# Routed attention with a SoLU block on one Trainium2 core: one pass of cluster products for two-token pairs, and a new order of all engines

## The chip, the cores and the metric

The kernel runs on one core of one Trainium2 chip. The metric is device time in microseconds, the median of repeated runs. The engines are PE (TensorE matmul; PEld is its weight load), DVE (VectorE), ACT (ScalarE), POOL (GpSimd) and SP (SyncE, which issues nearly all DMAs).

## The reference

Four batches of eight heads, 768 tokens of 64 numbers each. Every query and key is assigned to one of 16 centroids of its head, and a query attends only to keys of its own cluster. The result, 3072 rows of 512, goes through a block of width 1024. All inputs and the output are float32.

```python
q_assign = np.argmax(np.einsum('bhsd,hcd->bhsc', q_n, c_n), axis=-1)   # normalised q, k, centroids
k_assign = np.argmax(np.einsum('bhsd,hcd->bhsc', k_n, c_n), axis=-1)
mask = q_assign[:, :, :, None] == k_assign[:, :, None, :]
scores = np.where(mask, scale * np.matmul(q, k.transpose(0, 1, 3, 2)), -1000000000.0)
attn = np.exp(scores - np.max(scores, axis=-1, keepdims=True))
attn = attn / (np.sum(attn, axis=-1, keepdims=True) + 1e-09)
x = np.matmul(attn, v).transpose(0, 2, 1, 3).reshape(3072, 512)
h = x @ w_in
sm = softmax(h); solu = h * sm
ln = (solu - mean(solu)) / np.sqrt(var(solu) + 1e-06) * g_ln
return ln @ w_out
```

## The kernel before

Work goes by *pairs*: a batch `b` and two neighbouring heads, `b.p`, sixteen in all. For each pair the 64 numbers of a head lie along partitions, and below them one-hot marks of the token's cluster are appended, so that one product of marked keys and marked queries gives score plus a bonus for equal clusters; the exponential with a bias then does the masking. The marks of a pair's second head need their own rows, and marks of the other head there must be blank.

Steps have short names, followed by pair, operand (0 query, 1 key), head of the pair and half where there are any:

- `ld`, `lv`, `lo`, `li`, `lg`: loads of q and k, of v, w_out, w_in, g_ln. `tp`: tokens turned by PE into a bank of the PSUM region `hreg` (batch 0 only; the other batches are turned by `xt` on DVE). `xa`, `xb`: copies of what was turned to SBUF, tile `xt`. `ca`: cast of a head's part to the bfloat16 tile `qk`.
- `cl`: products of the turned tokens with the centroids into the PSUM tile `csc`. `tb` turns them back (`cst`), `mx` takes the largest of 16, `oh` makes the one-hot marks, `ot` turns these (`oht`), `pl` places a part of them into `qk` (a copy on POOL or DVE, or a DMA by SP), `bl` blanks a strip of the second head's key marks.
- `S`: one bank of scores (1 to 4 products); `E`: its exponential on ACT; `V`: products with v; `N`: division by the sum. A bank of scores goes to a ring of three PSUM tiles `sps`, or, for some early ones, to a bank of `hreg`.
- `ptx`, `tx`: x turned (by PE and copy, or by DMA); `h`: product with w_in into `hreg`; `hm`, `ex`, `u`: its largest, the exponential, the product h times exponential; `bn`, `ag`, `at`, `al`: the statistics and the scale `alpha`; `ptu`, `tu`: u turned; `y`: product with w_out; `sc`: scaling by alpha; `ou`, `oz`: the store.
- `su`, `me`, `ce`: the mean over rows of g_ln times w_out (DVE sums, a PE product) and w_out less it, which goes to `w_out_c`, the operand of every `y`. `wi`: casts of w_in. `cp`, `cb`, `cq`, `cf`: centroids turned, and their two forms kept as weights. `wm`, `fl`: idle products of PE during the opening.

Batch 0 is loaded with tokens contiguous in a partition. Its first pair goes by halves; its other three (`twelve` in the code) are loaded twelve tokens to a partition, so that a turn of 128 columns brings two tokens at once, one for each half of the partitions. Such a turned tile holds the even tokens of both heads in one half of the partitions and the odd ones in the other, and `cl` for these pairs uses weights with four variants `c_by_two` (part of the tokens by head), two products that add up for each of the four strips of `csc`, eight in all. An ordinary pair has four.

The order on every engine is written out by hand, as text: `ORDER["DVE"]` names kinds of step in the order in which they are issued, and each kind's steps come in the order in which they were added. `AWAY` lists steps that run on another engine than their default. An engine executes its own list strictly in order. Buffers that matter here: `hreg` has three banks, reused by `tp` and then by scores and `h`; unused parts of `w_out_c` hold small constants of the opening until `ce` fills it.

Of the kernel before, what the change touches and what calls it, by code (L numbers as in the profile page):

```python
# [10 lines left out]
F32 = mybir.dt.float32  # L11
BF16 = mybir.dt.bfloat16
# [10 lines left out]
class Weave:  # L23
# [6 lines left out]
        ld4 si ld3 lv lg ld3 lo lv lo ld2 lo2 lv ld6 lv ld8 li4 tx ld3 lv ld tx lv tu ld10 tx tu ld4  # L30
        tu lv ld ou lv ld3 tu ld3 ou ld8 ou2 ld2 tu ld5 tx lv2 ld pl tu ld10 tx ld5 ou2 tu lv tx lv
        tu ld9 ou tu ld4 lv2 ld4 pl tu ou tx ld3 tu tx ld4 ou tu2 ou lv tx lv ou pl3 tu3 ou tx2 ou2
        tu tx tu tx tu ou2 tx ou tu2 ou tu ou6
    """
    ORDER["POOL"] = """
        pl2 bl pl3 ca pl ca cv ca3 pl3 bl ca pl ca pl cv z2 pl3 ca bl z cv2 ca pl4 sg bl cv2 wi ca
        wi7 ca3 at pl4 z cv ca2 cv bl cv al pl2 ca3 at pl2 z bl ca3 al at al pl4 at ca cv ca cv ca
        cv al bl ca3 pl4 ca2 pl4 at2 pl2 bl ca cv pl al2 ca2 cv2 ca2 at cv ca4 al pl4 at2 cv bl cv3
        pl2 al pl2 ca2 bl ca at al ca pl2 cv2 pl ca3 al ca3 pl at2 pl3 al2 ca2 pl ca at cv pl cv at
        ca at cv al pl2 bl pl al at3 al2 at al2 at al at al2 at2 po at al3  # L40
    """
    ORDER["PE"] = """
        fl wm tp2 cp fl4 cl tp2 fl4 cl fl tp S2 cq S tp S tp S2 tp S tp2 S2 cl S V3 S2 tp3 S gt V3
        S2 tp2 S tp S2 cl S3 V3 S7 V3 S3 cl S3 V4 S5 V2 S V2 S4 V S2 V3 S cl S3 V2 S V S2 V S me S3
        V S V3 me S3 ptx V2 S2 cl V S V S5 V2 h4 S2 h V2 S3 h V2 S V2 S h S2 h S V S V2 S V S h S2 h
        V S2 V2 S y3 V S2 y S h2 S2 V2 h2 S2 cl S V S V2 S V S h S2 h S V S V S h y4 S3 V3 h2 S2 V2
        S h S2 V y S y3 S2 V2 S cl S V S V S V2 S2 y S y S2 V3 S2 y S V S y S2 V2 S h S2 V3 S2 cl S
        V3 S3 cl S2 V2 S V2 S h2 S3 h V S V S V2 y3 S2 y V S2 V h S2 V S h S V S h2 S3 h V2 S2 V4 h
        S3 y3 S2 V y S2 V3 S2 h2 S3 V2 cl S3 V2 h S2 h cl V2 S2 V2 S h S2 h2 S2 V3 y S y S y S y V S
        V2 S h2 S2 h2 S3 V3 S V y3 V y V S2 h S cl S3 V2 h S2 h V S2 V S cl V2 S3 y2 S V S V y2 h2  # L50
        S2 V2 S h2 S3 cl S V3 S V S2 y3 S2 V y V S h S2 h V2 S h2 S3 h V2 S y2 S V2 S2 V2 y2 S2 h3
        S3 V2 h2 V y S3 y3 V3 S3 h2 S2 cl S V S V S V2 S y2 h V S2 h V S2 h2 S2 V S V h V4 S2 y2 h
        S3 V2 h2 S2 V2 S y2 S2 h2 y2 S h2 S2 V2 y S V2 S y h2 S3 h2 S2 V4 y S3 h2 y V S2 h2 V S V S
        V y4 S2 V h4 S3 y V3 y S2 y2 h4 y S V3 y V y2 h ptx h y h2 y3 h2 y4 h2 ptu2 y8 ptu y4 ptu y4
    """
    ORDER["DVE"] = """
        cn xb cb tb mx oh ot pl2 tb mx oh ot xa3 cf ca bl cv tb mx oh ot ca2 xa gk su2 N tb mx xa oh
        cv ot su N su2 tb mx N oh su ot N xt2 N su tb mx su oh N xt2 N ce tx ce3 N ce4 hm N ot u N
        bn hm tb N mx oh bn ag ot u xt2 hm cv N bn u bn2 tb mx hm bn N oh ag2 u ot xt2 hm bn N sc u
        bn tb ag cv N xt mx oh xt ot sc N bl xt2 tb bn N mx ca tb N mx oh ot hm oh N ot u xt bn3 ag  # L60
        xt N ag hm sc N ca u bn2 xt bl sc hm ag N xt tb mx u tb oh ot N hm mx xt oh u bn2 ot N hm bn
        ag xt ca u N bn tb xt2 mx ag hm tb N bn2 oh ot u xt2 N hm tb mx oh N ag bn bl u mx bn ot N
        bn oh hm ot ag xt u N bn xt ag hm bn2 ag u sc N bl hm ca tb mx cv2 oh u ot N bn2 hm N bl u
        cv ag bn2 hm N bn u sc hm N u bn2 hm N bn ag u bn sc hm ag N bn u bn2 hm bn N ag2 u bn2 hm
        ag bn N ag2 u tx bn hm sc u bn2 hm tu2 bn ag2 u2 bn2 ag tu sc
    """
    ORDER["ACT"] = """
        wa xa2 ca2 xa2 xb ca4 E6 xa E2 xa E xa ca E3 xa3 E4 ca E2 xa E53 ex E13 ex E5 sc E3 ex E11
        ex E3 sc E5 ex E35 ex E15 ex E15 ex E9 ex E3 sc E8 ex sc E14 ex E sc E10 ex E5 sc E6 ex E5
        sc E3 ex ca E10 ex E9 ex E5 sc E2 ex E6 ex E7 ex E6 ex sc E5 ex E3 sc E ex sc ex sc ex sc2  # L70
        tu sc2 oz
# [3 lines left out]
        ca0.0.0.0.0 ca0.0.0.1.0 ca0.0.0.1.1 ca0.2.0.0 ca0.2.1.0 ca3.2.0.1 sc23.0 xa0.0.0.1 xa0.0.1.0  # L75
        xa0.1.1.1 xa0.2.0.0 xa0.2.0.1 xa0.2.1.0 xa0.2.1.1 xa0.3.0.0 xa0.3.1.0 xb0.0.1.1
    """.split(), "ACT"))
    AWAY.update(dict.fromkeys("""
        bl0.0.1 bl1.3 bl2.1 bl3.0 bl3.1 bl3.3 ca0.1.0.0 ca0.1.0.1 ca0.2.1.1 ca2.1.0.0 ca2.2.1.0
        ca3.0.0.1 ca3.3.1.0 cv0.0.0 cv0.1.0 cv1.1.0 cv1.2.0 cv3.1.1 cv3.2.1 cv3.3.0 pl0.0.0.0.1  # L80
        pl0.0.0.1.1 sc11 sc13 sc14 sc18 sc2 sc23.1 sc3 sc4 sc5 tu22.0
    """.split(), "DVE"))
    AWAY.update(dict.fromkeys("""
        ca0.0.1.1.1 pl0.0.0.0.0 pl0.0.0.1.0 pl0.0.1.0.0 pl0.0.1.1.0 pl1.0.0.0 pl1.0.0.1 pl1.0.1.0
        pl1.0.1.1 pl1.1.0.0 pl1.1.0.1 pl1.1.1.0 pl1.1.1.1 pl1.2.0.0 pl1.2.0.1 pl1.2.1.0 pl1.2.1.1
        pl1.3.0.0 pl1.3.0.1 pl1.3.1.0 pl1.3.1.1 pl2.0.0.0 pl2.0.0.1 pl2.0.1.0 pl2.0.1.1 pl2.1.0.0
        pl2.1.0.1 pl2.1.1.0 pl2.2.0.0 pl2.2.0.1 pl2.2.1.0 pl2.2.1.1 pl2.3.0.0 pl2.3.0.1 pl2.3.1.0
        pl2.3.1.1 pl3.0.0.0 pl3.0.0.1 pl3.0.1.0 pl3.1.0.0 pl3.1.0.1 pl3.1.1.0 pl3.1.1.1 pl3.2.0.0
        pl3.2.0.1 pl3.2.1.0 pl3.2.1.1 pl3.3.0.0
# [79 lines left out]
def kernel(  # L169
# [11 lines left out]
    nc = tc.nc  # L181
# [68 lines left out]
    def used(hh):  # L250

        return slice(0, D + NC_) if hh == 0 else slice(0, D + 2 * NC_)
# [222 lines left out]
    def clusters(b, p, hf, hh=None):  # L475

        lo, n = (0, HALF) if hf is None else (hf * HALF, QTR)
        if not hh:
            asg[b, p, hf, "csc"] = ps_m.tile([P, HALF], F32, name="csc", tag="m")
        csc = asg[b, p, hf, "csc"]  # L480
        if twelve(b, p):
            for c in range(4):
                i, part = divmod(c, 2)
                nc.tensor.matmul(csc[c * NB:(c + 1) * NB, :], c_by_two[:, p, 2 * part + hh, :],  # L484
                                 by_two(b, p, i)[:, hh].rearrange("p t n -> p (t n)"),
                                 start=(hh == 0), stop=(hh == 1), tile_position=(0, c * NB))
        for c in range(4) if not twelve(b, p) else ():
            i, part = divmod(c, 2)
            nc.tensor.matmul(csc[c * NB:(c + 1) * NB, :n], c_bd[:, p, :],  # L489
                             xts[b, p, i][:, lo + part * n:lo + (part + 1) * n],  # L490
                             tile_position=(0, c * NB))
        asg[b, p, hf, "n"] = n
# [25 lines left out]
    def assign_turn(b, p, hf):  # L518
        n = asg[b, p, hf, "n"]
        asg[b, p, hf, "oht"] = pr.tile([P, HALF], BF16, name="oht")  # L520
        nc.vector.transpose(asg[b, p, hf, "oht"][:, :n], asg[b, p, hf, "oh"][:, :n])  # L521
# [803 lines left out]
```

## Time and profile before

| what | value |
|---|---|
| median of three runs | 223.82 us (223.24, 223.82, 224.28) |
| span of the profiled execution, first to last instruction | 222.4 us |
| its whole time beside the span | not recorded; the median stands 1.4 us above the span |
| PE busy | 214.8 us (97%) |
| DVE, ACT, POOL busy | 199.1 (90%), 194.7 (88%), 126.6 us (57%) |
| granted PE clock over the span | 0.999 |

Busy time of an engine is the union of its instructions; that of PE includes the depth of its pipeline, so it overstates how full PE is. A row of the chain of work that ended last gives start, length and the engine, tile and line; "issue" is time in which the profile shows no cause. In a timeline row, "x6" merges six neighbouring instructions, and the bracket at its end gives the engine's idle time ahead of it and what ended it. "Q" names such as SPq are an engine's instruction queue.

### The profile page before, as it was taken

The numbers are of one execution on the slowest core, as the hardware profiler recorded it, in microseconds if no ns is written. First come the engines' busy times: TensorE is split into PE (matmuls) and PEld (weight loads), VectorE is DVE, ScalarE is ACT, GpSimd is POOL, SyncE is SP. The second block draws the span as 40 slices with busy tenths as digits, with TensorE's granted clock in tenths as the row PEclk, the third lists the DMA queues.
The fourth block names the chain that finished last, engine by engine and source line by source line (L and its number), as shares of the span: only waits on it lengthen the run. The fifth ranks groups of instructions, "written<-read, shape, count | busy, mean of one in ns | idle before, by whom it ended". The sixth has DMA issues, their size and how long they took to land.

```text
span 222.4 us, 6852 instructions
## 1 busy us (share of the span) xinstructions
PE 214.8 (97%) x2518; PEld 151.8 (68%) x2548; DVE 199.1 (90%) x363; ACT 194.7 (88%) x382; POOL 126.6 (57%) x252
## 2 busy tenths in 40 slices
PE   8999899999999999999999999999999999999993
PEld 7765577767777687777777666676767767665452
DVE  2789999999999999899989999999999979999891
ACT  3899999999999999999999989999999989795352
POOL 3189597759884986188837674783746101226131
PEclk9999999999999999999999999999999999999999
DMA  6998989797799979899999897998922928565623
GB/s 157 352 388 221 193 165 284 203 172 165 127 175 237 180 141 215 136 193 166 153 211 239 156 185 150 151 168 158 230 99 50 115 78 145 117 165 121 166 98 143
DMA packets 122433, 38.74 MB, mean 174 GB/s; under 512 B 111448, under 2 KB 117152, under 8 KB 122400
## 3 DMA queue, kind: packets, MB, share of 16 engines
q1 hardware_dynamic: 121680, 37.82, 79.8%
q10 hardware_dynamic: 720, 0.49, 0.7%
q8 instruction: 20, 0.33, 0.7%
q14 instruction: 13, 0.11, 0.1%
HBM read 23.11 MB, written 6.29 MB: 132 GB/s over the span
## 4 chain that ended last, share of the span: by engine, by line
PE 91%; DVE 3%; issue 2%; ACT 2%; DVEq 0%; ACTq 0%
PE sps L627 27%; PE hreg L744 18%; PE yps L813 17%; PE ops L654 16%; PE csc L489 4%; PE hreg L627 2%; PE idle_p L859 2%; PE csc L484 1%; PE hreg L403 1%; PE hreg L396 1%; ACT qk L468 1%; PE hreg L813 1%; ACT e L635 1%; DVE u L763 1%; DVE w_sum L598 1%
## 5 line engine op out<-in xcount | busy, mean ns | idle before, releaser
L635 ACT ACTIVATE e<-sps 128x512 bf16<-128x512 f32 (+1 forms) x276 | 143.2, 609 | 10.2 <-PE sps L627 9.8
L627 PE MATMUL sps<-qk 96*128 96x256 bf16 (+5 forms) x600 | 87.4, 263 | 0.7 <-ACT e L635 0.4
L627 PEld LDWEIGHTS <-qk 96*128 96x128 bf16 (+1 forms) x636 | 59.6, 121 | 24.5 <-issue 8.8
L654 PEld LDWEIGHTS <-e 128*128 128x128 bf16 x1152 | 49.9, 97 | 9.3 <-issue 1.9
L654 PE MATMUL ops<-v,e 128*128 128x65 bf16 x1152 | 54.3, 193 | 0.4 <-DVE x L679 0.4
L744 PE MATMUL hreg<-w_in_sb,xT 128*128 128x512 bf16 x177 | 48.3, 378 | 0.8
L813 PE MATMUL yps<-w_out_c,uT 128*128 128x512 bf16 x169 | 45.1, 379 | 0.8
L540 POOL COPY qk<-oht 32x384 f32<-32x384 f32 (+1 forms) x49 | 24.2, 494 | 21.5 <-DVE oht L521 15.7
L763 DVE TENSOR_TENSOR u<-e_sb,hreg 128x1024 bf16<-128x1024 bf16 (+1 forms) x25 | 29.1, 1169 | 2.7 <-ACT e_sb L756 2.1
L774 DVE BATCH_NORM_STATS2 bs<-u 128x6 f32<-128x512 bf16 x48 | 31.3, 677 | 0.0
L750 DVE TENSOR_REDUCE nmax<-hreg 128x1 f32<-128x1024 f32 x24 | 29.1, 1213 | 2.0 <-PE hreg L744 1.7
L756 ACT ACTIVATE e_sb<-hreg,nmax 128x1024 bf16<-128x1024 f32 x24 | 26.9, 1121 | 4.5 <-DVE nmax L750 4.4
L790 POOL TENSOR_SCALAR esq<-es,mv 128x1 f32<-128x1 f32 x24 | 8.3, 344 | 33.6 <-DVE mv L778 30.3
L813 PEld LDWEIGHTS <-uT 128*128 128x128 bf16 x200 | 18.0, 97 | 13.1 <-issue 0.3
L744 PEld LDWEIGHTS <-xT 128*128 128x128 bf16 x192 | 17.6, 97 | 11.3 <-ACT e L635 0.3
L472 POOL TENSOR_SCALAR qk<-xt 64x768 bf16<-64x768 f32 (+1 forms) x27 | 22.2, 823 | 3.5 <-DVE xt L444 1.7
L444 DVE STREAM_TRANSPOSE xt<-raw 128x768 f32<-128x768 f32 x24 | 22.2, 949 | 0.0
L470 POOL CAST qk<-xt 64x768 bf16<-64x768 f32 (+1 forms) x25 | 20.9, 836 | 1.2
L679 DVE TENSOR_TENSOR x<-ops,den 128x256 bf16<-128x256 f32 (+1 forms) x39 | 18.9, 486 | 1.3
L784 POOL TENSOR_SCALAR es<-esum 128x1 f32<-128x1 f32 x24 | 5.6, 236 | 20.9 <-ACT e_sb L756 20.4
L793 POOL TENSOR_TENSOR alpha<-esq,halves 128x1 f32<-128x1 f32 x24 | 13.8, 574 | 2.0
L830 ACT ACTIVATE y<-yps,alpha 128x512 f32<-128x512 f32 x15 | 10.4, 695 | 4.3 <-PE yps L813 3.0
(85 smaller groups left out, 206.9 us busy)
## 6 DMA issues: line engine op xcount, KB each, us to landing
vf<-in_v_dram SPq DMA_DIRECT2D x16, 384.0 KB, 4.6
out_dram<-y SPq DMA_DIRECT2D x23, 256.0 KB, 2.5
raw<-in_q_dram SPq DMA_DIRECT2D x50, 96.0 KB, 3.8
raw<-in_k_dram SPq DMA_DIRECT2D x50, 96.0 KB, 3.0
w_g<-in_moe_w_out_dram SPq DMA_DIRECT2D x4, 512.0 KB, 8.3
w_st<-in_moe_w_in_dram SPq DMA_DIRECT2D x4, 512.0 KB, 6.2
raw<-in_q_dram SPq DMA_DIRECT2D x3, 384.0 KB, 6.0
raw<-in_k_dram SPq DMA_DIRECT2D x3, 384.0 KB, 7.8
```

The source lines that it names most:

```text
L444: nc.vector.transpose(xt[:], raws[b, p, i][:].rearrange("p j c -> p (j c)"))
L472: VEC[e].tensor_scalar(dst, src, scalar1=inv_C, scalar2=1.0, op0=Alu.mult, op1=Alu.mult)
L540: ins = VEC[e].tensor_copy(dst.bitcast(F32), src.bitcast(F32).unsqueeze(1) .to_broadcast([NB, 2, n // 2]))
L627: ins = nc.tensor.matmul(sps_[n, k][:, c0:c0 + w], side(b, h // 2, 1, h % 2, keys)[r], side(b, h // 2, 0, h % 2, slice(s0 * P, s0 * P + w) ...
L635: ins = nc.scalar.activation(es[n, k][:, :w], sps_[n, k][:, :w], Act.Exp, scale=exp_scale, bias=-exp_scale)
L654: nc.tensor.matmul(opss[g][:, s, :VW], es[n, k][:, c0:c0 + P], v1[slot(b, h // 2)][:, h % 2, kt, :VW], start=(kt == 0), stop=(kt == n_t - 1))
L744: uses(nc.tensor.matmul(hreg[:, at(f, f2)[1], :], xTs[f][:, dc, :], w_in_sb[:, dc, f2 * FF2:(f2 + 1) * FF2], start=(dc == 0), stop=(dc == ...
L750: uses(nc.vector.tensor_reduce(ff[f, "nmax"][:], pair_of(f), axis=AXY, op=Alu.max, negate=True), *both(f))
L756: uses(nc.scalar.activation(ff[f, "e"][:], pair_of(f), Act.Exp, bias=ff[f, "nmax"][:], accum_out=ff[f, "esum"][:]), *both(f))
L763: uses(nc.vector.tensor_tensor(ff[f, "u"][:, r], ff[f, "e"][:, r], pair_of(f)[:, r], op=Alu.mult), *both(f)[r])
L774: nc.vector.bn_stats(ff[f, "bs"][:, f2, :], ff[f, "u"][:, f2, :])
L813: ins = nc.tensor.matmul(dst, ff[f, "uT"][:, at(f, f2)[0] * (n_fc // 2) + c, :], w_out_c[:, fc, cols], start=(fc == fcs[0] and turn == 0 i ...
```

## The change

For the three two-token pairs of batch 0, `cl` uses two weights (`c_two`, one for each head) and contracts over both token parities' partitions at once: a strip of `csc` belongs to a head's 32 marks, 16 for each parity, instead of to a parity's 32 marks, 16 for each head. Four products, one pass, no accumulation. `oh` writes the marks with the two parities parted: a strip `apart` of 128 x 768, zeroed once at the start, of which each group of 32 columns gets 16. `ot` then turns 768 columns instead of 384 into `turned_apart` (two buffers), and `pl` copies 16 rows by 768 marks into one head's rows instead of 32 by 384 into both heads'. Nothing needs a blank in these pairs, so their three `bl` are gone, and scores of their second heads contract over 80 rows instead of 96. Clearing of the four-variant mask (five POOL writes) becomes one write of `apart`; `cf` writes 256 columns instead of 512.

The text of `ORDER` is new for all engines and `AWAY` is new, as are some costs that the order does not depend on while it is written out. By the lists: SP issues 13 placements (before 5), POOL 51 (61), DVE 4 (2); DVE makes 8 of the twelve `xa` copies of the two-token pairs (5), ACT 4 (7); of casts DVE makes 4 whole ones and a half one (7 whole), ACT 3 whole and 1 half (3 and 6); DVE has 9 casts of v (7), 3 blanks (6) and 8 scalings of y with the two parts of the last (9 with one part). The first score bank must now stand behind all idle products.

```diff
     def clusters(b, p, hf):
         lo, n = (0, HALF) if hf is None else (hf * HALF, QTR)
-        if twelve(b, p):
-            for c in range(4):
-                i, part = divmod(c, 2)
-                nc.tensor.matmul(csc[c * NB:(c + 1) * NB, :], c_by_two[:, p, 2 * part + hh, :],
-                                 by_two(b, p, i)[:, hh].rearrange("p t n -> p (t n)"),
-                                 start=(hh == 0), stop=(hh == 1), tile_position=(0, c * NB))
+        csc = asg[b, p, hf, "csc"] = ps_m.tile([P, HALF], F32, name="csc", tag="m")
+        for c in range(4):
             i, part = divmod(c, 2)
+            if twelve(b, p):
+                w = c_two[:, p, part, :]
+                x = by_two(b, p, i)[:, part].rearrange("p t n -> p (t n)")
+            else:
+                w, x = c_bd[:, p, :], xts[b, p, i][:, lo + part * n:lo + (part + 1) * n]
+            nc.tensor.matmul(csc[c * NB:(c + 1) * NB, :n], w, x, tile_position=(0, c * NB))
...
     def assign_hot(b, p, hf):
+        if twelve(b, p):
+            dst = apart.rearrange("p (u a c) -> p a u c", u=2, c=NB)[:, :, :, :NC_]
+            src, top = (x.rearrange("p (a u) c -> p a u c", u=2)
+                        for x in (by_group(b, p, hf, "cst"), spread_max(b, p, hf)))
...
     def assign_turn(b, p, hf):
+        if twelve(b, p):
+            asg[b, p, hf, "oht"] = turned_apart[:, p % 2, :]
+            nc.vector.transpose(turned_apart[:, p % 2, :], apart)
+            return
...
         if twelve(b, p):
-            ins = VEC[e].tensor_copy(
-                every_other(b, p, i, part)[D:D + NB].bitcast(F32),
-                src.bitcast(F32).rearrange("p (t n) -> p t n", t=n_t // 2).unsqueeze(1)
-                .to_broadcast([NB, 2, n_t // 2, P // 2]))
+            dst = (side(b, p, i, part, slice(0, S))[D:D + NC_].bitcast(F32)
+                   .rearrange("p (t u n) -> p u t n", u=2, n=P // 2))
+            src = asg[b, p, hf, "oht"][r.start:r.start + NC_, :].bitcast(F32)
+            ins = VEC[e].tensor_copy(dst, src.rearrange("p (u t n) -> p u t n", u=2, n=P // 2))
...
     ORDER["PE"] = """
-        fl wm tp2 cp fl4 cl tp2 fl4 cl fl tp S2 cq S tp S tp S2 tp S tp2 S2 cl S V3 S2 tp3 S gt V3
+        fl3 wm fl tp2 cp fl tp cq tp fl2 cl fl tp2 fl cl tp fl tp2 S3 cl S2 tp S tp S2 tp S tp S gt
...
```

The places that matter for the time are shown as the engines' lists. First DVE in batch 0, where the second and third pairs' clusters and the last `xa` copies stand (L430 is `xa` before, L433 after; L595 and L598 are `su` before, L605 and L608 after; `w_out_c` as both result and source is the parted strip). Before:

```order
L430 COPY xt<-hreg 128x384
L588 COPY g_ln_115<-gps 128x8
L595 TENSOR_SCALAR w_sum<-w_g,g_ln_115 128x512
L598 SCALAR_TENSOR_TENSOR w_sum<-w_g,g_ln_115,w_sum 128x512
L666 RECIPROCAL den<-ops 128x6
L679 TENSOR_TENSOR x<-ops,den 128x2x3x64
L497 STREAM_TRANSPOSE cst<-csc 128x384
L510 TENSOR_REDUCE mx<-cst 128x24
L430 COPY xt<-hreg 128x384
L515 TENSOR_TENSOR oh<-cst,mx 128x384
```

After:

```order
L433 COPY xt<-hreg 128x384
L495 STREAM_TRANSPOSE cst<-csc 128x384
L527 STREAM_TRANSPOSE w_out_c<-w_out_c 128x768
L508 TENSOR_REDUCE mx<-cst 128x24
L676 RECIPROCAL den<-ops 128x6
L689 TENSOR_TENSOR x<-ops,den 128x2x3x64
L433 COPY xt<-hreg 128x384 x2
L521 TENSOR_TENSOR w_out_c<-cst,mx 128x12x2x16
L433 COPY xt<-hreg 128x384
L605 TENSOR_SCALAR w_sum<-w_g,g_ln_115 128x512
```

The first two `su` steps stood ahead of the last `xa` copy and now follow it; the wide turn stands ahead of it.

Second, ACT in the same place, from the first exponential on (L635 is `E` before, L645 after; L468 and L471 are casts). Before:

```order
L635 ACTIVATE e<-sps 128x384 x6
L430 COPY xt<-hreg 128x384
L635 ACTIVATE e<-sps 128x384 x2
L430 COPY xt<-hreg 128x384
L635 ACTIVATE e<-sps 128x384
L430 COPY xt<-hreg 128x384
L468 ACTIVATE qk_101<-xt 64x6x128
L635 ACTIVATE e<-sps 128x384 x3
L430 COPY xt<-hreg 128x384 x3
```

After:

```order
L433 COPY xt<-hreg 128x384 x4
L645 ACTIVATE e<-sps 128x384 x9
L471 ACTIVATE qk_101<-xt 64x6x128
L645 ACTIVATE e<-sps 128x384 x15
L645 ACTIVATE e<-hreg 128x512 x2
```

The four copies left to ACT stand ahead of its first exponential; of the seven before, all stood among the exponentials.

Third, DVE at the very end, with the last `tu` copy (L738 before, L748 after) and the scalings (L832, L842). Before:

```order
L763 TENSOR_TENSOR u<-e_sb,hreg 128x512 x2
L774 BN_STATS bs<-u 128x6 x2
L778 BN_AGGR mv<-bs 128x2
L738 COPY uT<-utp 128x512
L832 TENSOR_SCALAR w_in_sb<-hreg,alpha 128x192
```

After:

```order
L773 TENSOR_TENSOR u<-e_sb,hreg 128x512
L788 BN_AGGR mv<-bs 128x2
L784 BN_STATS bs<-u 128x6
L788 BN_AGGR mv<-bs 128x2
L748 COPY uT<-utp 128x512
L842 TENSOR_SCALAR y<-yps,alpha 128x512
L842 TENSOR_SCALAR w_in_sb<-hreg,alpha 128x320
L842 TENSOR_SCALAR w_in_sb<-hreg,alpha 128x192
```

The next-to-last row block's scaling and both parts of the last one now stand on DVE in a row.

## Prediction before the run

> **What bounds the kernel now.** First the page's busy totals and the table of stretches, to see which engine has no room:
>
> ```profile
> span 222.4 us, 6852 instructions
> PE 214.8 (97%) x2518; PEld 151.8 (68%) x2548; DVE 199.1 (90%) x363; ACT 194.7 (88%) x382; POOL 126.6 (57%) x252
> ...
> 0.00:10.00 10.00, 9.03 (x162) 7.46 (x163) 4.61 (x20) 5.32 (x12) 2.99 (x20) 1.00 0.77 237
> ...
> 20.00:30.00 10.00, 9.22 (x127) 5.80 (x127) 9.68 (x20) 9.52 (x21) 7.24 (x12) 1.00 0.93 213
> 30.00:40.00 10.00, 9.79 (x149) 7.47 (x147) 9.46 (x18) 10.00 (x22) 8.13 (x18) 1.00 0.96 247
> ...
> 60.00:70.00 10.00, 9.94 (x110) 7.05 (x110) 9.78 (x19) 9.54 (x20) 6.10 (x11) 1.00 1.10 165
> ```
>
> The columns of a stretch are its length, then busy time of PE, PEld, VectorE, ScalarE and GpSimd, the granted clock, the DMA share and GB/s. From 30 us on PE is busy 9.8 to 9.9 of 10, so the end is set by how much PE has to do. Only the opening has holes (9.03, and 9.22 between 20 and 30). Second, the chain of work that ended last says who makes those holes:
>
> ```profile
> 13.68 1.43 PE csc L484 x16
> ...
> 19.68 0.82 DVE w_sum L595
> 20.52 1.19 DVE w_sum L598
> ...
> 23.40 0.56 DVE xt L430
> ...
> 24.09 0.60 PE hreg L627 x4
> ...
> 32.22 0.30 issue
> ...
> 34.45 0.78 PE csc L489 x8
> ...
> 48.98 0.42 issue
> ```
>
> Columns are start, length, and what. The chain leaves PE near 19 us for five microseconds of VectorE: the first product of batch 0's second pair (24.09, into a bank of hreg) waits for the last copy of turned tokens out of that bank (xt, 23.40 to 23.96), and VectorE reached that copy only after two w_sum steps, a normalise and a second pair's cluster chain. Call the arrival of that product, 24.09, the milestone. After it the chain is PE nearly throughout, with small waits for ScalarE such as the two issue rows.
>
> **The change part by part.** *One pass of cluster products.* A two-token pair's cl is 16 rows and 1.43 us (the csc L484 row); an ordinary pair's, with half the products, is 8 rows and 0.78 us (the csc L489 row). Three pairs change from the one to the other: 3 x 0.65 = 1.95 us off PE. PE work is what the end follows, so this is on the path wherever PE doesn't just wait longer instead: two of the three (1.3 us) lie ahead of the milestone, where VectorE decides, one (0.65) behind it.
>
> *VectorE up to the milestone.* The new order puts all w_sum steps behind the last xt copy. These are the rows that price the stretch:
>
> ```profile
> 7.38 0.38 DVE L497 STREAM_TRANSPOSE cst<-csc 128x192 f32<-128x192 f32 x1 [1.13 <-PE csc L489]
> ...
> 9.60 0.38 DVE L497 STREAM_TRANSPOSE cst<-csc 128x192 f32<-128x192 f32 x1
> ...
> 11.10 1.45 DVE L430 COPY xt<-hreg 128x384 f32<-128x384 f32 x3
> ...
> 15.17 0.58 DVE L497 STREAM_TRANSPOSE cst<-csc 128x384 f32<-128x384 f32 x1 [0.71 <-PE csc L484]
> ...
> 16.97 0.58 DVE L521 STREAM_TRANSPOSE oht<-oh 128x384 bf16<-128x384 bf16 x1
> ...
> 18.11 0.81 DVE L472 TENSOR_SCALAR qk<-xt 64x768 bf16<-64x768 f32 x1
> 19.01 0.58 DVE L430 COPY xt<-hreg 128x384 f32<-128x384 f32 x1
> ...
> 21.63 0.18 DVE L666 RECIPROCAL den<-ops 128x6 f32<-128x6 f32 x1
> ...
> 22.32 0.57 DVE L497 STREAM_TRANSPOSE cst<-csc 128x384 f32<-128x384 f32 x1
> L444 DVE STREAM_TRANSPOSE xt<-raw 128x768 f32<-128x768 f32 x24 | 22.2, 949 | 0.0
> L540 DVE COPY qk<-oht 32x192 f32<-32x192 f32 x2 | 0.5, 270 | 0.1
> ```
>
> In the new order VectorE has, from the first tb to the last xt copy: the first half's chain with two placements (7.38 to 9.60, 2.22), the second half's chain (9.60 to 11.10, 1.50), two more placements (0.54), eight xt copies instead of five (seven at 0.52, between 0.48 each in the run of three and 0.58 alone: 3.64; the eighth with the small copy gk, 19.01 to 19.68, 0.67), tb, mx and oh of two whole pairs (15.17 to 16.97, 1.80 each: 3.60), one wide turn ot, one cast (0.81) and one normalise (21.63 to 22.32, 0.69). The wide turn of 128x768 in two-byte numbers isn't in the trace; 128x384 costs 0.58 in two-byte numbers and 0.58 in four-byte ones (the rows at 16.97 and 15.17), so the type has not counted and I take the 128x768 row's 0.95; bounds 0.58 and 1.16 (twice a 128x384). Sum 2.22 + 1.50 + 0.54 + 3.64 + 0.67 + 3.60 + 0.95 + 0.81 + 0.69 = 14.62 us.
>
> It starts when the first cl is done. There the new PE order puts the second half's turns and a repeat of the centroids' turn ahead of that cl, and takes four idle products away:
>
> ```profile
> 5.92 0.85 PE idle_p L859 x8
> 6.78 0.53 PE csc L489 x8
> 7.31 0.55 PE hreg L396 x24
> ...
> 11.45 0.33 PE hreg L403 x3
> 10.61 2.34 ACT L635 ACTIVATE e<-sps 128x384 bf16<-128x384 f32 x6
> L468 ACT ACTIVATE qk<-xt 64x768 bf16<-64x768 f32 x3 | 2.5, 849 | 0.1
> ```
>
> The turns are 0.55 more, the idle products 0.43 less (0.85 for eight); they may have filled a wait for the data, or not, so the start is 0 to 0.55 later. I take the middle, 7.65 instead of 7.38. The last xt copy then ends at 22.3 instead of 23.96: the milestone comes 1.65 us earlier. With the ends of the unknowns (start 0.27 either way, copies 0.28, ot 0.37 less or 0.21 more) it ends between 21.4 and 23.0, a gain of 0.9 to 2.6.
>
> Who could be late instead? ScalarE: from its first e on it owes 24 of them at 0.39 (2.34 for six) and one cast (0.85), 10.2 us, where it now has seven xt copies among them; that ends under 22.3 while the first e starts before 12.1. It starts at 10.61 now; PE gets four more turns ahead of the first scores, 0.33 each, so 11.9 at the latest: just covered, and if VectorE were quicker than 22.1, ScalarE would be next. GpSimd: the second pair's marks are turned at 18.7 by the same terms (7.65, then the two chains and placements 4.26, four copies 2.08, tb, mx and oh 1.80, gk, cast and copy 1.42, the third pair's tb 0.57, ot 0.95), and three placements must follow.
>
> ```profile
> L533 POOL COPY qk<-oht x12: 497/614/934, 17.7 to 34.5; 32x384 f32<-32x384 f32 x12
> ```
>
> The new placement has 16 rows for 32, and the same 384 words in each: I take 0.614, bounds 0.497 and 0.934, so they are done at 20.6, at the worst 21.5, under VectorE's 22.3. The three blanks that go were GpSimd's and are worth nothing there while this cover holds. [...]
>
> *Clearing and marks.* The zeroed strip and smaller own-mask are GpSimd work before its idle wait for the first marks; cf shrinks from 512 to 256 columns and falls into VectorE's 1.13 us wait ahead of 7.38. The score products of odd heads contract over 80 rows for 96; rows do not set their time (275 and 274 ns):
>
> ```profile
> L627 PE MATMUL sps<-qk 80*128 80x256 bf16 x216 | 35.9, 275 | 0.6 <-ACT e L635 0.4
> L627 PE MATMUL sps<-qk 96*128 96x256 bf16 x216 | 35.5, 274 | 0.0
> SPq L538 <- DVE den L666: 9.1, 1, 9.1
> L538 SPq DMA_DIRECT2D qk<-oht x5: 586/622/753, 96.1 to 169.8; - x5
> 218.79 0.53 ACT L830 ACTIVATE w_in_sb<-hreg,alpha 128x320 f32<-128x320 f32 x1 [0.87 <-PE hreg L813]
> 219.13 0.42 DVE L832 TENSOR_SCALAR w_in_sb<-hreg,alpha 128x192 f32<-128x192 f32 x1 [1.40 <-PE hreg L813]
> ```
>
> *The rest of the order.* Totals hardly move: by instruction counts VectorE gains three copies, a cast of half a pair, three wide turns and loses three casts, three blanks and two y scalings; ScalarE loses five half casts and three xt copies and gains two y scalings, GpSimd loses ten placements that go to SP or VectorE. With PE at 9.9 of 10 and no engine heavier, I cost the reshuffle of batches 1 to 3 at nothing. Its cover is the room in the others (VectorE 0.2 to 0.5 of 10); were that gone, PE would wait as at 48.98, 0.3 to 0.5 us a time; the bounds are four such waits more (+1.7), or the two shown gone (-0.7). At the end both last scalings stand on VectorE, one behind the other, where ScalarE had one: 0.53 and 0.42 now end at 219.55; in a row from 218.79 they end at 219.74: +0.2.
>
> **Sum.** -1.65 (milestone, two cl inside) - 0.65 (third cl) + 0.2 (end) = -2.1 us. The profiled span is 222.4; its total beside that isn't given, and the median of the runs, 223.82, stands 1.4 above the span. The same 1.4 kept: 223.82 - 2.1 = 221.7. Its own range follows the milestone's bounds, 220.8 to 222.5. A run differs from another by 1.04 in 224, so 0.5%, 1.1 us, is about what can be told from no change.
>
> **Rivals.** *Given back in the middle* (no change that can be measured). Eight w_sum steps now stand behind the milestone instead of six; at 0.81 and 1.19 that is 2.0 us more for VectorE, plus 2 x 0.38 of wide turns, in a stretch where it is 9.46 to 9.68 of 10 busy. For: the mean of w_out's rows, its centring and every y wait for the last of these. Against: the new PE order puts the mean's product after 59 score banks instead of 54. If half of it (1.4) comes back as PE waiting: 223.1.
>
> *The placements on the SP queue* (slower). Before, 5 placements go by DMA, now 13. Each issue holds the in-order queue until its marks are turned (the 9.1 us row is one such wait, harmless there), then 0.62 to issue, with the loads and the turned u and x behind it. PE has now no wait for a turned tile. It decides once a held queue makes uT or xT land after PE reaches its y or h; eight more such heads at 0.5 us of PE wait (the size of 48.98) are +4.0, less 2.1: 225.7. Against: the waits of SP shown cost PE nothing.
>
> *More than forecast*: the milestone at its lower bound (21.4, with ScalarE's first e then needed by 11.2) and the ScalarE waits gone, -0.9 - 0.7: 220.1.
>
> *The clock.* It is granted at 1.00 in all the stretches shown, the opening with its idle products included. The new order waits there for data with fewer idle products behind it. If the clock fell to half over what follows such a wait (5.92 to 7.86 on the chain now), that would take 1.9 us more: 223.6. [...]
>
> **How the numbers follow.** Forecast 0.50, given back 0.22, SP 0.12, more than forecast 0.14, the clock 0.02. The range runs from 219.8 to 224.2: it takes in the forecast, the better case with 0.3 below it for its far side, and the given-back case up to half of what it could cost more, and leaves out most of the SP case. Faster by over 0.5% (under 222.7): nearly all of the forecast, the better case and a tenth of the rest, 0.66. Within: most of the given-back case, the clock, the edge of the SP case, 0.23. Slower (over 224.9): 0.11.
>
> **What would show it.** Right: csc rows of 0.78 only, none of 1.43; the first product into hreg near 22.3, with no w_sum on the chain ahead of it; the wide turn near 0.95; PE's busy time near 213; the last scaling in a row on VectorE. Wrong: the milestone still at 24, with ScalarE or GpSimd on the chain ahead of it; PE waiting for w_out_c, uT or xT between 35 and 60 us; an SP wait on a placement with PE idle behind it; holes in PE beyond 60 us.

## The result, and the profile after

The changed kernel takes 232.73 us (median of 4 runs, 231.80 to 233.01), the kernel before on the same chip 223.70 (4 runs, 223.24 to 224.28). The ratio is 1.039, with a 95% interval of 1.036 to 1.042: 9 us slower, where 2 us faster was forecast and 224.2 was the range's end. The profiled execution spans 231.1 us against 222.4, at a granted clock of 0.997; the clock stands at 1.00 from 4.5 to 229.8 us, so none of the loss is the clock's. Here and below a time is the median of all runs, and a ratio with its interval leaves out runs over 1.5% longer than the kernel's fastest (two of e1's ten, one each of e7's and e12's four).

The chain of work that ended last, by engine, on the page of before:

```profile
PE 91%; DVE 3%; issue 2%; ACT 2%; DVEq 0%; ACTq 0%
```

From the page of after, the busy times and the same chain, by engine and by line:

```profile
PE 217.8 (94%) x2524; PEld 150.5 (65%) x2524; DVE 203.1 (88%) x364; ACT 194.5 (84%) x375; POOL 125.4 (54%) x243
...
PE 70%; DVE 15%; DMA 5%; issue 3%; ACT 3%; POOL 2%; SPq 1%; DVEq 0%; POOLq 0%; ACTq 0%
PE sps L637 19%; PE hreg L754 16%; PE yps L823 14%; PE ops L664 11%; PE csc L489 4%; DMA raw<-in_k_dram 4%; DVE w_sum L608 3%; ACT e L645 3%; DVE xt L447 2%; PE idle_p L869 2%; DVE x L689 1%; DVE mx L508 1%; DMA raw<-in_q_dram 1%; DVE oh L521 1%; DVE u L773 1%
```

No engine got heavier by much. But PE has only 70% of the chain for 91%; loads of k, the sums of `w_out` and the turn `xt` of raw tiles stand on it now. Three stretches (columns: window, its length, then busy us and instructions of each engine, clock, DMA share, GB/s), first of before, then of after:

```profile
0.00:40.00 40.00, 37.90 (x539) 27.83 (x539) 32.57 (x75) 34.80 (x78) 26.53 (x62) 1.00 0.90 256
40.00:160.00 120.00, 118.50 (x1376) 85.94 (x1393) 113.83 (x198) 114.31 (x223) 81.42 (x146) 1.00 0.94 176
```

```profile
0.00:40.00 40.00, 35.81 (x508) 25.61 (x508) 34.15 (x75) 31.95 (x69) 31.41 (x63) 1.00 0.94 263
40.00:160.00 120.00, 114.53 (x1327) 81.31 (x1328) 108.39 (x190) 110.22 (x212) 72.56 (x129) 1.00 0.94 171
160.00:231.00 71.00, 67.45 (x692) 43.60 (x689) 60.58 (x101) 52.37 (x97) 21.46 (x52) 0.99 0.49 114
```

In the middle, where nothing of the algorithm was changed, PE went from 1.5 us idle in 120 to 5.5. Busy time hides the start of each wait in the pipeline's depth (before's products of 256 columns last 275 ns on the mean and start 109 apart in the median), so I also add up waits from the starts of PE's matmuls: the time to the next start beyond 0.42 ns a column (what an undisturbed row takes: 0.108 us for 256 columns, 0.215 for 512), where that is over 0.06 us, with the waits inside a `cl`. Gaps of the 0.22 us that a record missing from the trace leaves are not counted.

| PE's waits, us | 0 to 40 | 40 to 160 | behind | all |
|---|---|---|---|---|
| before | 3.3 | 1.5 | 0.3 | 5.1 |
| after | 6.9 | 7.9 | 0.6 | 15.4 |

10.3 us more waiting, less 1.95 for three shorter `cl`, leaves 8.35; the last product starts 8.56 us later (227.33 against 218.77). So the sum closes: no work was added, the kernel lost it by waiting, a third in the opening, the rest in batches 1 to 3. (How the first rows of a `cl` are counted moves up to 1 us between the first two columns, and the totals by 0.4.)

The largest waits in the middle have one pattern. SP's queue, then VectorE, then PE of after (start, length, engine, tile; the bracket is idle time ahead and its end's cause; L548 is a placement, L563 a load of v, L439 a load of q or k):

```profile
59.59 0.57 SPq L439 DMA_DIRECT2D raw<-in_k_dram  x1
60.26 0.77 SPq L548 DMA_DIRECT2D qk<-oht  x1
61.12 0.53 SPq L563 DMA_DIRECT2D vf<-in_v_dram  x1
61.70 0.45 SPq L439 DMA_DIRECT2D raw<-in_k_dram  x1
```

```profile
65.41 0.98 DVE L447 STREAM_TRANSPOSE xt<-raw 128x768 f32<-128x768 f32 x1 [1.57 <-issue]
...
93.16 0.98 DVE L447 STREAM_TRANSPOSE xt<-raw 128x768 f32<-128x768 f32 x1 [2.01 <-DMA raw<-in_k_dram]
```

```profile
65.55 1.73 PE L489 MATMUL csc<-xt,c_bd 128*32 128x384 f32 x8
...
94.66 0.85 PE L489 MATMUL csc<-xt,c_bd 128*32 128x384 f32 x8 [1.74 <-DVE cst L495]
```

The last quarter of a k tile is issued at 61.70, behind a placement and a load of v, and lands at 65.33. VectorE comes to this tile's `xt` at 63.8 and stands; the `cl` that needs it takes 1.73 us for 0.85. At 93.16 another `xt` waits so; behind it on VectorE stands the turn back of the last `cl`, so the next one starts 1.74 us late at 94.66. A third is at 134.96. VectorE's waits of after for a raw tile (us in all, times, longest), of which before had none; the "issue" row is the one that ends at 65.41, 0.08 us behind the landing:

```profile
DVE xt L447 <- DMA raw<-in_k_dram: 4.5, 2, 2.5
...
DVE xt L447 <- issue: 1.6, 1, 1.6
```

Over the 24 raw tiles of batches 1 to 3 the mean time from landing to `xt` fell from 5.5 us (least 1.8) to 2.8 (least 0.08). By the lengths of its rows SP's queue is occupied for 91.5 of the 100 us from 60 to 160, before for 86.0.

### The profile page after: what moved, and what is told of

The parts are those of the page before. It is cut to its first block, busy times and chain, and to the rows that moved or that the text cites. A ratio compares the mean times of both kernels' runs of the same rounds, so it can differ in the third digit from the quotient of the medians.

```text
span 231.1 us, 6825 instructions
## 1 busy us (share of the span) xinstructions
PE 217.8 (94%) x2524; PEld 150.5 (65%) x2524; DVE 203.1 (88%) x364; ACT 194.5 (84%) x375; POOL 125.4 (54%) x243
## 4 chain that ended last, share of the span: by engine, by line
PE 70%; DVE 15%; DMA 5%; issue 3%; ACT 3%; POOL 2%; SPq 1%; DVEq 0%; POOLq 0%; ACTq 0%
PE sps L637 19%; PE hreg L754 16%; PE yps L823 14%; PE ops L664 11%; PE csc L489 4%; DMA raw<-in_k_dram 4%; DVE w_sum L608 3%; ACT e L645 3%; DVE xt L447 2%; PE idle_p L869 2%; DVE x L689 1%; DVE mx L508 1%; DMA raw<-in_q_dram 1%; DVE oh L521 1%; DVE u L773 1%
## 5 line engine op out<-in xcount | busy, mean ns | idle before, releaser
L645 ACT ACTIVATE e<-sps 128x512 bf16<-128x512 f32 (+1 forms) x276 | 144.2, 604 | 13.8 <-PE sps L637 12.5
L637 PE MATMUL sps<-qk 80*128 80x256 bf16 (+5 forms) x600 | 94.3, 264 | 1.9 <-POOL qk L543 0.8
L637 PEld LDWEIGHTS <-qk 80*128 80x128 bf16 (+1 forms) x636 | 60.6, 121 | 32.1 <-issue 7.9
L664 PEld LDWEIGHTS <-e 128*128 128x128 bf16 x1152 | 52.9, 97 | 13.1 <-DVE x L689 2.9
L664 PE MATMUL ops<-v,e 128*128 128x65 bf16 x1152 | 58.6, 193 | 1.3 <-DVE x L689 0.8
L754 PE MATMUL hreg<-w_in_sb,xT 128*128 128x512 bf16 x192 | 53.9, 379 | 1.8 <-DMA xT<-x 0.9
L823 PE MATMUL yps<-w_out_c,uT 128*128 128x512 bf16 x184 | 50.2, 379 | 0.1
L550 POOL COPY qk<-oht 32x384 f32<-32x384 f32 (+1 forms) x39 | 19.2, 492 | 27.7 <-DVE oht L530 23.9
L760 DVE TENSOR_REDUCE nmax<-hreg 128x1 f32<-128x1024 f32 x24 | 29.1, 1212 | 4.3 <-PE hreg L754 4.1
L773 DVE TENSOR_TENSOR u<-e_sb,hreg 128x1024 bf16<-128x1024 bf16 (+1 forms) x25 | 29.1, 1165 | 1.7 <-ACT e_sb L766 1.6
L473 POOL CAST qk<-xt 64x768 bf16<-64x768 f32 (+1 forms) x30 | 24.8, 828 | 4.7 <-ACT xt L425 3.3
L475 POOL TENSOR_SCALAR qk<-xt 64x768 bf16<-64x768 f32 (+1 forms) x29 | 23.1, 796 | 3.0 <-DVE mv L788 1.1
L840 ACT ACTIVATE y<-yps,alpha 128x512 f32<-128x512 f32 x17 | 11.8, 692 | 5.0 <-PE yps L823 4.4
L803 POOL TENSOR_TENSOR alpha<-esq,halves 128x1 f32<-128x1 f32 x24 | 13.7, 569 | 2.0
L568 POOL CAST v<-vf 128x384 bf16<-128x384 f32 x23 | 12.0, 529 | 4.8 <-PE csc L489 2.2
```

What stands on the lines that cost most here:

```text
L473: VEC[e].tensor_copy(dst, src)
L475: VEC[e].tensor_scalar(dst, src, scalar1=inv_C, scalar2=1.0, op0=Alu.mult, op1=Alu.mult)
L637: ins = nc.tensor.matmul(sps_[n, k][:, c0:c0 + w], side(b, h // 2, 1, h % 2, keys)[r], side(b, h // 2, 0, h % 2, slice(s0 * P, s0 * P + w) ...
L645: ins = nc.scalar.activation(es[n, k][:, :w], sps_[n, k][:, :w], Act.Exp, scale=exp_scale, bias=-exp_scale)
L664: nc.tensor.matmul(opss[g][:, s, :VW], es[n, k][:, c0:c0 + P], v1[slot(b, h // 2)][:, h % 2, kt, :VW], start=(kt == 0), stop=(kt == n_t - 1))
L754: uses(nc.tensor.matmul(hreg[:, at(f, f2)[1], :], xTs[f][:, dc, :], w_in_sb[:, dc, f2 * FF2:(f2 + 1) * FF2], start=(dc == 0), stop=(dc == ...
```

## The experiments

*Algorithm or lists?* e1 is the new code with the old lists, e2 the reverse.

```diff
 e1: after, with ORDER and AWAY of before
-    bl0.1 bl0.2 bl0.3            (POOL; nothing to blank)
 e2: before, with ORDER and AWAY of after
+    bl0.1 bl0.2 bl0.3            (POOL, behind pl0.p.1.*)
```

e1: 

> One pass of cluster products, with the engines' lists and the choice of engines of the kernel before (its three blanks of two-token pairs dropped). Theory 'order': the loss of 9 us sits in the new lists, and the one pass itself is worth its three saved cl steps less a wider oh (1.05 for 0.56) and a wider turn (0.94 for 0.58) on VectorE: 221.5 to 224.5. Rival 'marks': the wide marks and turns make batch 0's pairs late and everything behind them: 228 or more.

e2: 

> The two-pass clusters and 32-row placements of the kernel before, with the new lists (three blanks put back on GpSimd behind the key placements). Theory 'order': as slow as the changed kernel or a little slower, 232 to 236. Rival 'marks': the narrow oh and turn bring most of it back, 224 to 228.

e1 takes 224.64 us, ratio to before 1.003 (1.001 to 1.006); e2 237.12, ratio 1.058 (1.051 to 1.064). The lists make the loss: 8.1 us with the one pass, 13.2 without it. The clock has a part of the 13.2: in e2's trace it is granted at 0.50 from 34.2 to 37.6 and from 44.4 to 47.9 us, behind PE waits of 3.1 and 1.7 us; 6.8 us at half speed cost at most 3.4 (an estimate). But the one pass alone gained nothing either: in e1 PE waits 5.4 us up to 40 us, before 3.3, which is about what three `cl` save.

*Is it the loads, or SP's placements?* e3 moves the loads, e4 the placements, e5 both.

```diff
 e3  ORDER["SP"] of after: from ld1.2.0.0 on, every ld 5 to 6 entries ahead
 e4  ORDER["SP"]   - pl1.1.1.1 pl1.2.1.0 pl2.0.0.0 pl2.1.1.0 pl2.1.0.0 pl2.1.0.1 pl2.3.1.1 pl3.1.1.1
     ORDER["POOL"] + the same eight, each beside its pair's others
 e5  both
```

e3: 

> The changed kernel; only SP's list differs: from the third pair of batch 1 on each load of q or k goes 5 to 6 entries further ahead, past stores, placements, turned tiles and v loads. Theory 'late loads': the three waits of VectorE's xt for a raw tile (8.5 us in all on its queue) go and with them most of the PE gaps of 1 to 1.9 us that they make: 227 to 229.5. Rival 'SP is full': what is moved back (turned u and x, placements) is late instead: 231.5 to 234. Rival 'the late loads cost nothing': 232 to 233.

e4: 

> The changed kernel with 8 of the 13 placements that SP makes (so many as the new lists added) put on GpSimd among their neighbours, 8 x 0.61 us there and 8 x 0.63 us less on SP. Theory 'SP is full': the loads behind them come 0.6 us earlier for each one passed, the xt waits shrink by half or more: 228 to 231. Rival 'order elsewhere': no change or a little slower, 232 to 234.

e5: 

> The two edits of e3 and e4 together: 8 placements off SP and the loads 5 to 6 entries ahead. Theory 'SP is full and in order': with the placements gone the loads can go ahead without making the turned tiles late, the xt waits vanish and the PE gaps between 60 and 160 us (about 6 us in the changed kernel, 4 to 5 in e3 and e4) fall under 2.5: 228 to 229.5. Rival 'the tables of the other engines hold it': no better than e3 or e4 alone, 230.5 to 232.

e3 231.02 us (ratio 1.030, 1.025 to 1.036), e4 231.42 (1.033, 1.029 to 1.037), e5 230.72 (1.031, 1.029 to 1.034): 1.3 to 2.0 us better than after, e3 and e4 only just (after's interval begins at 1.036, where theirs end). None is what its theory of SP promised; e3 and e4 lie between the ranges of their theories, e5 in that of its rival. In e4 VectorE's waits for raw tiles are halved:

```profile
DVE xt L447 <- DMA raw<-in_k_dram: 1.6, 2, 1.3
DVE xt L447 <- issue: 1.5, 1, 1.5
```

But PE then waits 1.1 us for a placement and 0.8 for a cast on GpSimd, which got the eight. In e3 VectorE has no wait for a raw tile left; PE's waits of e3 (engine, tile, cause: us in all, times, longest) say what is late instead:

```profile
PE sps L637 <- POOL qk L543: 2.0, 3, 1.2
PE hreg L754 <- DMA xT<-x: 1.8, 2, 1.5
PE yps L823 <- DMA uT<-u: 1.3, 2, 1.0
```

The turned x and u, which the loads passed. (The first row belongs to the opening, which e3 doesn't edit; in after it is 0.8.) So "SP is full" holds there in kind, though the time lies under its range. In e5 neither is late; PE's waits of e5:

```profile
PE sps L637 <- POOL qk L550: 1.1, 1, 1.1
...
PE sps L637 <- POOL qk L543: 0.8, 2, 0.5
...
PE hreg L614 <- DVE w_sum L608: 0.8, 1, 0.8
PE sps L637 <- POOL qk L475: 0.8, 1, 0.8
```

Now GpSimd's placements (L550) and the casts queued behind them (L475) are late. From 40 to 160 us PE waits 4.7 us, after 7.9; under 2.5 was forecast, and the profiled execution, 229.4, is the fastest of e5's four. The mean time from a raw tile's landing to its `xt` is about 5.7 us in e3 and 7.8 in e5, no less than the 5.5 of before. So late raw tiles, with SP's placements, hold about 2 of the 9 us.

*Opening or rest?* The lists are cut at about 46 us.

```diff
 e6  all lists: after's up to S19 / N8 / E19, then before's
 e7  all lists: before's up to h0 / ce6 / E18, then after's
```

e6: 

> The new lists of all engines up to about 46 us (S19 on PE, N8 on VectorE, E19 on ScalarE), and then the lists of the kernel before. Theory 'two losses' (PE gaps of the changed kernel: 3.6 us more in the opening, 5.8 more behind it, cl 2 less): the opening alone gives 225 to 226.5. Rival 'the opening is the cause': 230 or more. Rival 'the opening gains': 223 or less.

e7: 

> The reverse: the lists of the kernel before up to about 46 us (with one pass), and then the new ones. Theory 'two losses': 5 to 7 us over e1: 229.5 to 231.5. Rival 'the opening is the cause': 224 to 226.

e6 229.58 us (ratio 1.028, 1.024 to 1.031), e7 231.42 (1.031, 1.027 to 1.035). e7 came out as expected: the new rest costs 6 to 7 us over e1. e6 missed, 3 us over its range: 3.5 us of PE waits stand between 40 and 60 us, at and behind the cut, probably since the old rest assumes work that the new opening has not yet done there. That trace is of e6's longest execution, 231.67, with the clock at 0.50 from 42.6 to 46.0 us; the other three take 229.5 without it, so the clock doesn't make the miss. The opening's own share can't be read from e6; from e7 against after it is 1.3 us by the medians, 1.9 by the ratios.

*What SP's list alone does to a good order.* e8 first, a mended e1 (below); e11 and e12 put after's SP traits into it.

```diff
 e11  ORDER["POOL"] of e8 - the eight placements of e4
      ORDER["SP"]         + the same, where GpSimd made them
 e12  ORDER["SP"] of e8: loads, stores and turns in after's order, 5 placements kept
```

e11: 

> e8 with 8 more placements on SP (those of batches 1 to 3 that the changed kernel has there), taken from GpSimd and put where GpSimd made them. Theory 'SP is nearly full and in order': 8 x 0.63 us more on a queue that is 88% busy between 60 and 150 us delays loads and turned tiles: 225 to 228, with PE waits for raw, uT or xT that e8 hasn't. Rival 'only their place in the new lists is at fault': 223.4 to 224.4.

e12: 

> e8 with SP's loads, stores and turns in the order of the changed kernel, and the 5 placements of the kernel before. All other lists are e8's. Theory 'each load has little lead and the new order takes it': VectorE's xt waits for raw tiles and PE behind them, 226 to 229. Rival 'the order of SP is harmless, it is the number of its transfers': 223.4 to 225.

e11 226.57 us, ratio 1.014 (1.012 to 1.016): 2.9 over e8 by the medians, 3.4 by the ratios. The time is as forecast, the waits for raw, uT or xT are not there. PE's largest new wait, for a placement that lands late:

```profile
PE sps L634 <- DMA qk<-oht: 1.5, 1, 1.5
```

(The line numbers of this kernel are lower by three.) Another 0.7 us, for a cast of v on GpSimd, is new too. e12 takes 250.02 us (1.115, 1.112 to 1.118), far beyond what either theory gave. VectorE waits for raw tiles of k, as the first theory has it (7.3 us). PE's waits of e12:

```profile
PE ops L664 <- DVE x L689: 4.2, 2, 3.3
PE csc L489 <- DVE xt L447: 2.6, 1, 2.6
PE sps L637 <- ACT e L645: 2.5, 3, 1.7
PE hreg L614 <- DVE w_sum L608: 2.4, 1, 2.4
```

A good part of the 26 us is the clock. In e12's trace it is granted at 0.50 in four stretches, 23.9 us in all, the longest from 29.1 to 42.8 us, within and behind a PE wait of 3.3 us for `x`; over the whole span it is 0.95 to 0.96 in all four runs. At half speed that costs up to 12 us (an estimate). But the other half too is more than the 9 us that SP's order loses together with its own partners: a list that is put among others meets none of the leads it was written for, and the waits are passed on (VectorE's 7.3 us for raw tiles, PE's 2.6 for an `xt`). How much of after's loss is "SP's order" is therefore no number by itself.

*Can the one pass pay?* In e1 PE waited at three places for a VectorE step that stood behind sums of `w_out`.

```diff
 e8  ORDER["DVE"] of e1:
-    xa0.3.0.1 gk su0 su1 N0 tb0.2 mx0.2 xa0.3.1.1 oh0.2 cv0.1.0 ot0.2 su2 N1
+    xa0.3.0.1 xa0.3.1.1 gk N0 su0 tb0.2 mx0.2 oh0.2 ot0.2 su1 su2 N1
-    oh0.3 su5 ot0.3
+    oh0.3 ot0.3 su5                      (cv0.1.0 goes to POOL, ahead of pl0.2.1.0)
 e9  ORDER["DVE"] of e8:  gk ahead of xa0.3.0.1;  N3 ahead of ot0.3 and su5
 e14 e8's lists, clusters and blanks of before
```

e8: 

> e1 (one pass, old lists) with VectorE's list mended at the three places where PE waited in it: the last xa copy and the first division go ahead of the sums of w_out (0.40 and 0.59 us of PE waits at 23.9 and 22.3), the third pair's turn ahead of a sum (1.36 us at 33.6), one cast of v to GpSimd, which idled 2.7 us there. Theory 'VectorE's order sets the opening': 222 to 223.4. Rival 'VectorE is full from 20 to 50 us, so it comes back later' : 223.7 to 225.

e9: 

> e8 with two more moves on VectorE: the small copy gk ahead of the last two xa copies (the second pair's cl waited 0.40 us for it at 19.9) and a division ahead of the third pair's turn and a sum (PE waited 0.98 us for it at 32.4). Theory 'VectorE's order sets the opening': 222.4 to 223.3. Rival 'ScalarE, with hardly a gap from 10 to 35 us, holds it': 223.4 to 224.

e14: 

> e8's lists with the two-pass clusters and the three blanks of the kernel before: e8 less the one pass. Theory 'the one pass is worth its cl steps' (0.65 each, one or two of them on the path): 224.3 to 225.6 against e8's 223.7. Rival 'it gives back on VectorE and GpSimd what it saves on PE': 222.8 to 223.9, no slower than e8.

e8 takes 223.66 us, ratio to before 0.9988 (0.9979 to 0.9998): the only kernel below before, by 0.3 us. e14 has 223.89, ratio 1.0006 (0.9997 to 1.0015). e14 lies in the rival's range. One pass is thus worth 0.2 us by the medians, 0.4 by the ratios, under these lists; under after's it is 4.4 (e2 less after), of which e2's clock has up to 3.4. PE's waits tell why it is so little: 6.0 us in e8, 4.65 in e14. Most of what `cl` no longer fills, PE waits: e8 has 1.4 us of waits for VectorE's `x`, e14 none, and on VectorE the wide turn of the third pair stands ahead of the longer of the two. e9 was a miss: 224.73 us, ratio 1.0048 (1.0036 to 1.006). Of the waits it aimed at, 1.4 and 0.4 us, 0.4 are left, but `cl` of batch 1 then waits 0.5 for an `xt`; from 32 us on every step is 0.5 us later than in e8, up to the last product. The profiled span is 1.0 longer: at the end VectorE's last scaling starts 0.70 us behind the start of the last product, in e8 0.35. Why it does stays open.

*The long marks.* In e1 the same instruction, the parted `oh` of the three two-token pairs, took 1.10, 0.55 and 1.20 us. VectorE and GpSimd of e1 at the first two:

```profile
15.62 1.10 DVE L521 TENSOR_TENSOR w_out_c<-cst,mx 128x384 bf16<-128x384 f32 x1
...
23.67 0.55 DVE L521 TENSOR_TENSOR w_out_c<-cst,mx 128x384 bf16<-128x384 f32 x1
```

```profile
14.59 1.73 POOL L475 TENSOR_SCALAR qk<-xt 64x768 bf16<-64x768 f32 x2
16.27 1.14 POOL L473 CAST qk<-xt 64x768 bf16<-64x768 f32 x1
...
21.95 0.82 POOL L473 CAST qk<-xt 64x768 bf16<-64x768 f32 x1
```

GpSimd's second L475 cast began at 15.49, and the `oh` of 15.62 ends 1.23 after that: the cast's 0.83 and the 0.55 of an `oh` alone, but for 0.15. The cast that follows is stretched in its turn, 1.14 for 0.82. At 23.67 GpSimd is idle. In e8 an `oh` that began 0.13 us before the end of a cast took 0.56 (at 22.03), one that began 0.69 before it 1.09 (at 15.27). e10 asks whether the parted write has a share.

```diff
-            dst = apart.rearrange("p (u a c) -> p a u c", u=2, c=NB)[:, :, :, :NC_]
+            dst = apart[:, :HALF].rearrange("p (a u c) -> p a u c", u=2, c=NC_)
```

e10: 

> e8 with the marks of the two-token pairs written as 384 columns in a row and not parted (they then stand in the wrong places, so the scores are other ones; the work is the same). In e8 the three oh took 1.09, 0.56 and 0.64 us. Theory 'GpSimd': the long one stood behind a GpSimd cast that had begun 0.14 us before it, so dense writes keep the three times within 0.1. Rival 'the parted write is dear': all three fall to 0.55 and the time by 0.5.

One run, 223.8 us; the three `oh` of e10:

```profile
15.53 1.11 DVE L521 TENSOR_TENSOR w_out_c<-cst,mx 128x384 bf16<-128x384 f32 x1
22.30 0.56 DVE L521 TENSOR_TENSOR w_out_c<-cst,mx 128x384 bf16<-128x384 f32 x1
29.46 0.65 DVE L521 TENSOR_TENSOR w_out_c<-cst,mx 128x384 bf16<-128x384 f32 x1
```

In e8 they were 1.09, 0.56 and 0.64. The write pattern made 0.02 us at most, as theory 'GpSimd' had it.

*Do the opening and SP make the whole loss?* e13 joins e8's opening to e5's rest.

e13: 

> The opening of e8 up to about 46 us, then the new lists with both SP edits of e5. Theory 'opening and SP are the loss': 224.5 to 227. Theory 'the other engines' lists hold a part too, since each wait taken away uncovers the next': 227.5 to 230, with PE waits on GpSimd's casts and placements.

228.71 us, ratio 1.023 (1.020 to 1.025). The second theory had it. Of the 9 us, 4 are recovered; 5 stay in the lists of batches 1 to 3, where SP's has a part still (uT below). PE's waits of e13, the first of them in the opening, the others in the middle:

```profile
PE ops L664 <- DVE x L689: 1.4, 2, 1.0
PE yps L823 <- DMA uT<-u: 1.1, 1, 1.1
PE sps L637 <- POOL qk L550: 1.1, 1, 1.1
...
PE sps L637 <- POOL qk L475: 0.8, 1, 0.8
PE sps L637 <- ACT e L645: 0.6, 1, 0.6
```

The first is in e8 too. The other four make 3.6 of the 5 us, and more than half of that is GpSimd's placement and cast. Which steps of the lists make them late was not separated further.

## Why the prediction was wrong, step by step

**The step that failed: "the rest of the order", costed at nothing** with +1.7 as its bound. It measured 6 to 7 us (e7 against e1), with the opening +8.1 (after against e1). Step by step, by the medians: the one pass under the old lists +0.9 (e1), the new rest +6.8 (e7), the new opening +1.3 (after), where -2.1 was forecast for all. Its reasoning was that the engines' totals hardly move. Nor did they move much: 217.8 against 214.8, 203.1 against 199.1, 194.5 against 194.7 us. But totals tell nothing of a moved list. The bound was taken from two waits that the old lists showed, and the old lists were those that had been fitted to their own lead times. What could have been read is the lead, the time from a load's landing to its first use: in the old trace a raw tile landed 1.8 to 13 us ahead of its `xt`, and in the lists one can count what stands between a load and that `xt` now. The order of SP showed 8 more placements and the loads behind them. That would have warned, but not sized it: with the raw tiles' lead restored (e3, e5) 7 of the 9 us stay, and what PE waits for then are GpSimd's placements and casts and the turned u.

**The rival "placements on the SP queue"** had the right side and place, with a chance of 0.12 and 225.7 us. In a good order its price is 2.9 to 3.4 us (e11), near the 4.0 it assumed; in after the eight placements are worth 1.3 (e4). It decided by other means than it said: in after not uT or xT were late (0.9 us of waits for xT) but raw tiles of k, half of it through the placements (e4) and the rest through the loads' own order (e3), and in e11 the placement itself.

**The milestone** came at 23.28, a gain of 0.81 for 1.65, just under the lower bound of 0.9. PE and VectorE of after there:

```profile
23.28 0.60 PE L637 MATMUL hreg<-qk 80*128 80x256 bf16 x4 [0.55 <-DVE xt L433]
```

```profile
22.59 0.55 DVE L433 COPY xt<-hreg 128x384 f32<-128x384 f32 x1
```

The last `xt` copy still ends the wait, as forecast, but it ends at 23.14 for 22.3. Of these 0.84 us, 0.55 are the start: VectorE's first turn started at 8.20 for 7.65 (the bound was 7.93). The stretch itself took 14.94 us for 14.62: two of its marks took 0.98 and 0.86 for 0.55 and the cast 1.07 for 0.81, while other steps came out shorter and in part made up for it. And the 0.81 were lost again by 40 us: between 30 and 40 PE is busy 8.23 us for 9.79, with waits for GpSimd's placements and VectorE's `x` and `w_sum`. The groups of after that the step used (busy us, mean ns):

```profile
L521 DVE TENSOR_TENSOR w_out_c<-cst,mx 128x384 bf16<-128x384 f32 x3 | 3.2, 1053 | 0.0
L543 POOL COPY qk<-w_out_c 16x384 f32<-16x384 f32 x12 | 7.4, 618 | 1.1 <-DVE w_out_c L527 0.4
L608 DVE SCALAR_TENSOR_TENSOR w_sum<-w_g,g_ln,w_sum 128x512 f32<-128x512 f32 x7 | 6.8, 967 | 0.1
L527 DVE STREAM_TRANSPOSE w_out_c<-w_out_c 128x768 bf16<-128x768 bf16 x3 | 2.8, 940 | 0.0
L489 PE MATMUL csc<-xt,w_out_c 128*32 128x384 f32 x24 | 2.6, 498 | 0.5 <-DVE g_ln L598 0.5
```

The wide turn (0.95 forecast, 0.94) and the 16-row placement (0.614, 0.618) were right, and so was a `cl` at 0.78: its last row starts 0.65 us sooner than in two passes. The marks were not: 1.05 us for the 0.55 of before's rows that began with GpSimd idle, beside a fill of its, or within 0.15 us of its instruction's end. The prediction allowed for a spread of rows on GpSimd's side alone, in its bounds for a placement (0.497 to 0.934). VectorE's `oh` has one too: it took 1.10 us in e1 and 1.09 in e8 where a GpSimd cast had 0.70 and 0.69 us left, and 0.56 in before where GpSimd began a fill 0.06 us behind it (at 55.19).

**The third cl, -0.65**, was counted as plain gain. e14 against e8 shows that all three together are worth 0.2 to 0.4 us when the lists are the same: the opening is VectorE's, which gets 3 x 0.38 of turn, and GpSimd's, beside whose casts and placements marks and sums took longer (in e8 1.09 for 0.55 us, and two sums at 25.76 1.89, where one with GpSimd idle, at 36.13, took 0.74).

**Given back in the middle**: right in kind (the mean's product waits 0.8 us for `w_sum`, and seven of its sums took 967 ns on the mean for 837), too small by far as the whole story.

**The tail** was as forecast (from the start of the last product to the end of the span 3.8 us for 3.6), and so was **the clock** of after (1.00 up to the last product). The drop to half behind the opening's first wait, which a rival at 0.02 costed at 1.9 us, is not in its trace; of all traces those of e2, e6 and e12 alone have drops to 0.50 with products still to come, of 3.4 us each and one of 13.7. ScalarE's first e came at 11.53, within its 11.9.

## What to carry to other kernels

When a change replaces the order of in-order queues, don't cost the part outside its aim at nothing because totals stay: list for each load, placement and cast how far ahead of its first use it is done now, and what the new lists put between. A lead of 2 us is used up by three or four entries on a queue such as SP's here (an estimate from its rows of 0.45 to 0.77 us in after, where it is occupied for 91.5 us of 100). Mending one list then uncovers the next: e5 recovers 2 of the 9 us and e13 4. And take the duration of a VectorE step such as `oh` from rows beside the GpSimd work that it will meet, not from its row in a quiet place (here 1.05 us on the mean for 0.55); a product saved on PE is worth little while VectorE ends the stretches (0.2 to 0.4 us for 1.95 here).

## What the runs showed of the hardware that was not expected

VectorE's two-input `oh` of 128x384 took 0.55 us with GpSimd idle (before at 23.86) and up to 1.32 beside its casts (after at 28.68), 1.10 when it began 0.13 us behind one of 0.83 (e1 at 15.62); the GpSimd cast that followed took 1.14 for 0.82. With 0.15 us or less of GpSimd's instruction left it took 0.56 (before at 16.38, e8 at 22.03), and a GpSimd copy that came 0.03 us behind it took 0.88 for 0.50 (before at 94.5). Not every row of GpSimd's goes with a longer `oh`: one that began 0.14 us behind an `esq` of 128x1 and 0.81 us took 0.54 (after at 85.06). Writing the result of `oh` in runs of 16 elements in place of 384 in a row made 0.02 us at most (1.09, 0.56, 0.64 in e8 against 1.11, 0.56, 0.65 in e10). A turn of 128x768 took 0.94 us in two-byte numbers and 0.96 in four-byte ones (after, means of 3 and 24).

The granted clock fell to 0.50 within PE waits or up to 2.3 us behind them, for 3.4 us at a time and once for 13.7 (e2 twice, e6 once, e12 four times; waits of 1.1 to 3.5 us from one matmul's start to the next). Not every such wait did it: 2.0 us in after at 92.7 and 2.6 in e12 at 137 left the clock at 1.00. So the length of the last wait alone doesn't tell it. From run to run the kernel before took 223.1 to 224.4 us, after 231.8 to 233.0, e3 229.2 to 231.9, and e1, with the old lists, 224.1 to 232.7; no run shows what makes the spread.
